# A new hand order for batch 0 of a fused attention and MLP kernel, with small jobs on other engines

## The chip, the cores and the metric

The kernel runs on one core of a Trainium2 chip. The metric is the device time of one execution in microseconds. A core has five instruction streams: TensorE (PE in the profile, its weight loads PEld), VectorE (DVE), ScalarE (ACT), GpSimd (POOL) and SyncE (SP, which here only issues DMAs). Each works through its own queue in order and waits on semaphores for the others. ACT and POOL issue DMAs as well.

## The reference

Eight batches of attention (8 heads, 576 positions, head size 64) with a band of 32 positions to each side and 8 global positions, followed by a residual MLP over the 512 features:

```python
def _attn_ref(q, k, v, global_idx):
    ...
    scores = scale * np.matmul(q, k.transpose(0, 1, 3, 2))
    mask = np.abs(pos[:, None] - pos[None, :]) <= window
    mask = mask | is_global[:, None] | is_global[None, :]
    scores = np.where(mask, scores, -1000000000.0)
    ...
    return np.matmul(attn, v)

def _moe_ref(x, alpha1, beta1, w_tok, alpha2, beta2, w_ch1, w_ch2, lam):
    a1 = alpha1 * x + beta1
    tok = np.einsum('ts,bsd->btd', w_tok, a1)
    u = x + lam * tok
    a2 = alpha2 * u + beta2
    ch = np.maximum(a2 @ w_ch1, 0.0) @ w_ch2
    return u + lam * ch
```

All inputs and the output are float32; the indices are whole numbers.

## The kernel before

The 8 x 576 rows make nine groups of 512 rows for the channel MLP. The first is batch 0's rows 0 to 511. While TensorE runs the MLP of group g, the attention and the token mixing of the next batch are woven between its matmuls at fixed places (`weave`). Batch 0 has no MLP to hide in. Its attention and token mixing come first, as a list of some 190 named steps in the string `FIRST` (line 45), written in the order in which they are issued. A step may carry the number of its PSUM bank, as in `tk0:1`. The order of the string is the order of each engine's queue: a step waits for everything before it on the same engine. The order and the engines were found by a solver outside the kernel; nothing in the kernel decides them at run time. The table `ops` (line 916) says what a step does, and the strings `CK, QV, KC, QC, NY, PZ` (line 915) give the engine of a family of steps for each pair of heads (A is ACT, D is DVE, P is POOL).

The steps that matter here, h being a pair of heads:

- `ck`, `cq`: cast k and q of batch 0 from float32 to bfloat16 (lines 618, 621); `tk`, `tq`: transpose them on TensorE; `kt`, `qv`: copy them from PSUM. `tt`, `ktt`, `qtt`: the same for the last 64 positions.
- `V0` to `V4` (POOL, line 220): loads of the five overlapping chunks of V of batch 0 into `Ve[0]`; `va1`, `vb1`, `va2`, `vb2`: copies shifted by 64 partitions into `Vo[0]`. `u0` to `u4`: the loads of V for batch 1.
- `vez`: three small fills of `Ve[0]`; `v1f`: fills of `Ve[1]` and `KT[1]` for batch 1; `pz`: zero fills of the probability tiles; `qz0`, `qz1`: zero fills of the padded query tile `QP` of batch 1, 64 partitions by 1296 float32 each; `fz`, `ktz`, `pgz`, `kgz`: other fills.
- `s`, `e`: scores and their exponentials (line 361); `pg`, `pt`: masked probabilities (lines 323, 330); `q`, `ra`, `rd`: the rows of the global positions, on TensorE, ACT (line 383) and DVE (line 387); `pvx`, `pvy`: probabilities by V on TensorE, which need `rd`; `nx`, `nr`, `ny`: division by the row sums; `xl`, `xm`: multiplication by alpha1, on POOL for pairs 0 to 2 and on DVE for pair 3.
- `la`, `lb`, `lc`: lam times alpha1, spread over the partitions; `beta`: lam times beta1 in one row (line 860).
- `wki`, `wi`: loads of w_tok and w_ch1 (POOL); `wt`, `we`: transposes of w_tok and their copies; `rs`, `re`: its row sums.
- `tm`, `ad`, `tx`, `ut`: token mixing of one pair, its residual sum (DVE), transposes, and the scaled copy (ACT, line 901) that the channel MLP reads.
- `W1s`: the first nine matmuls of the first MLP group.
- `kc`, `qc`: casts of k and q of batch 1 (lines 618, 621); `gc1`: the global columns of batch 1 in `KGP` and `QP` (lines 242, 248).
- `gat1` (`ld_const`, line 731): SP copies two numbers out of `Ve[0]` into `A2`. The copy has no use as data, but SP waits in it until that chunk of V has landed. Then SP issues four loads of batch 1, k heads 0 to 3, q heads 0 to 3, k heads 4 to 7, q heads 4 to 7 (line 613), into the place where batch 0's k and q stood.
- `sp:n`: n matmuls without use.

After the string, `first_attention(1)` is woven into the first group: transposes of pair 0 of batch 1 (line 632), copies into `QP` by DVE (line 642) and into `KT` by ACT (line 636), the tail, pair 1, then score units, with MLP matmuls between. The PSUM banks 5, 6 and 7 are used in turn, so the pair 1 transposes of q wait for pair 0's copies, and so on.

Of the kernel before, what the change touches and what calls it, by code (L numbers as in the profile page):

```python
# [9 lines left out]
FP32 = mybir.dt.float32  # L10
# [6 lines left out]
P = 128  # L17
S = 576
D = 64
H = 8  # L20
HP = 4
# [3 lines left out]
NW = 9  # L25
# [18 lines left out]
]  # L44
FIRST = """
kgz vez io ktz pgz gb1 gbm:0 W0 gbc ar0 pz1 ar1 gath ck0 ar2 pgc tk0:1 sp:3 cq0 mask idn tq0:2 sp:16 V0 pz3 GM
qv0 V1 pz2 cq1 V2 tq1:3 kt0 cq2 V3 tq2:4 sp:1 ck2 qv1 qv2 ck1 tk2:5 V4 kt2 ck3 tk1:6 wki cq3 gat1 kt1 tk3:0 wi
kt3 gx tq3:2 ct qv3 gt:1 tt:3 sp:3 ge0 gte fz ktt ge1 qtt z20:4 s20:5 gk1:6 e201 la e200 z21:0 z11:2 s11:1
gk0:3 b1t eg1 va1 s21:5 e111 z00:4 s00:6 eg0 z10:1 sp:2 va2 e210 s10:3 vb1 G e211 z01:0 sp:2 e001 s01:5 e100
lb:6 e011 pz0 e010 pg2 z31:1 s31:5 lc v1f pt2 ab:0 sp:2 e310 q2:6 e000 u0 wt1:1 ra2 wt3:4 sp:2 we1 pg0 u1 rd2  # L50
pvx2:6 e101 vb2 pt0 e311 u2 pvy2:1 e110 q0:3 nx2 we3 wt0:5 u3 pg1 ra0 wt2:2 nr2 ny2 we0 wt4:6 xl2 rd0 we2 q1:4
pt1 z30:1 s30:5 pvx0:3 we4 xm2 pvy0:2 nx0 ra1 rs:6 e300 beta rd1 e301 nr0 pg3 pvy1:1 re pvx1:3 ny0 pt3 xl0
q3:4 tm2:5 ra3 nr1 ny1 rd3 xm0 nx1 pvy3:6 pvx3:2 ad2 xl1 tm0:4 nx3 xm1 nr3 ad0 ny3 tx2:3 u4 tm1:5 xl3 b1i xm3
tx0:4 ad1 tm3:6 abe ut0 qz0 ut2 tx1:5 ad3 qz1 ut1 tx3:4 gc1 ut3 W1s qc1 kc1 qc0 kc0 qc3 kc2 kc3 qc2
"""
PLACE = {t: (g, j) for g, ts in enumerate(GROUPS) for j, t in enumerate(ts)}

# [41 lines left out]
def kernel(ctx, tc, q, k, v, global_idx, alpha1, beta1, w_tok, alpha2, beta2, w_ch1, w_ch2, lam, out):  # L99
    nc = tc.nc  # L100
# [8 lines left out]
    def T(name, shape, dt):  # L109
        return cp.tile(list(shape), dt, name=name)  # L110
# [14 lines left out]
    def mm(o, l, r, st, sp):  # L125
        nc.tensor.matmul(out=o, lhsT=l, rhs=r, start=st, stop=sp, skip_group_check=True)  # L126
# [14 lines left out]
    QP = T("QP", [P, HP, 2, NW, 72], BF16)  # L141
    Vef = [T(f"Ve{i}", [P, 5 * H * 65], FP16) for i in range(2)]
    Ve = [t.rearrange("p (c h e) -> p c h e", c=5, h=H) for t in Vef]
    Vo = [T(f"Vo{i}", [P, 4, H, 65], FP16) for i in range(2)]
# [5 lines left out]
    G = T("G", [P, 2, 704], FP16)  # L150
    GM = T("GM", [P, 2, S], FP16)
# [14 lines left out]
    mask = T("mask", [P, NW, 64], FP16)  # L166
    gqm = T("gqm", [P, 5, 8], FP16)
    LA1 = T("LA1", [P, DM], FP32)
    LAM = T("LAM", [P, DM], FP32)
    A2 = T("A2", [P, DM], FP32)  # L170
# [12 lines left out]
    gbc = T("gbc", [P, 8], FP32)  # L183
# [113 lines left out]
    def gk0_mm(ps, t0, nt):  # L297
        for hp in range(HP):
            o = ps[:, 0 : 64 * nt].rearrange("p (t j) -> p t j", j=64)
            mm(o, KGP[:, hp, :], Q0[:, hp, t0 : t0 + nt, 0:64], hp == 0, hp == HP - 1)  # L300
# [305 lines left out]
    def fill(ap, val=0.0, eng=None):  # L606
        (eng or nc.vector).memset(ap, val)
# [4 lines left out]
    def ld_kq(src, st_, eng, b, h0, h1):  # L612
        eng.dma_start(
            out=st_[:, h0:h1, :, :].rearrange("p h j d -> p h (j d)"), in_=src[b, h0:h1, 0:512, :].rearrange("h (p j) d -> p h (j d)", j=4)
        )
# [53 lines left out]
    def tail_k(ps, b):  # L669
        tv = ps.bitcast(BF16)[:, 0:512].rearrange("p (i t) -> p i t", i=4)  # L670
        nc.scalar.copy(out=KT[b % 2][:, :, 544:608], in_=tv[:, :, 0:64])
# [7 lines left out]
    def tail_q0(ps, copy):  # L679
        tv = ps.bitcast(BF16)[:, 0:512].rearrange("p (i t) -> p i t", i=4)  # L680
        copy(out=Q0[:, :, 8, 0:64], in_=tv[:, :, 64:128])
# [31 lines left out]
    zero = nc.const_aps.tensor(0.0, (P, 1), FP32)  # L713

    g_ = nc.gpsimd
# [13 lines left out]
    nc.sync.dma_start(out=abr[4:8, :], in_=alpha2.rearrange("(c p) -> c p", p=P))  # L729

    def ld_const():
        nc.sync.dma_start(out=A2[0:1, 0:1], in_=Ve[0][0:1, 3, 0, 0:2].bitcast(FP32))
        for h0 in (0, 4):
            ld_kq(k, KST, nc.sync, 1, h0, h0 + 4)
            ld_kq(q, QST, nc.sync, 1, h0, h0 + 4)
        for t_, src in ((A2, alpha2), (LAM, lam)):
            nc.sync.dma_start(out=t_, in_=src.unsqueeze(0).to_broadcast([P, DM]))
# [2 lines left out]

    def qzero(a, eng):
        r = slice(64 - 64 * a, 128 - 64 * a)
        fill(QP.rearrange("p h a t j -> p h a (t j)").bitcast(FP32)[r, :, a, :], 0.0, eng)

    def ld_w2(blk):
        g_.dma_start(out=W2[:, 8 * blk : 8 * blk + 8, :], in_=w_ch2[1024 * blk : 1024 * blk + 1024, :].rearrange("(c p) e -> p c e", p=P))
# [14 lines left out]
    def ve_fill(i, eng=g_):  # L761
        fill(VF[i][0:32, 0:260], 0.0, eng)
        fill(VF[i][96:128, 1040:1300], 0.0, eng)
        fill(Ve[i][:, :, :, 64:65], 1.0, eng)

    def kt_fill(i, eng):
        fill(KT[i][:, :, 0:32], 0.0, eng)
        fill(KT[i][:, :, 608:672], 0.0, eng)
# [89 lines left out]
    def b0_beta(par, eng):  # L858
        r = 64 if par == 0 else 0
        eng.tensor_tensor(out=XL4[par][r : r + 1, :], in0=LB[r : r + 1, :], in1=LR[r : r + 1, :], op=ALU.mult)  # L860
# [45 lines left out]
    def ab_ev(ps):  # L906
# [4 lines left out]
    V_ = nc.vector  # L911
    mlp0 = mlp(0)
    hb = {}
    CPY = {"A": nc.scalar.copy, "D": nc.vector.tensor_copy, "P": nc.gpsimd.tensor_copy}
    CK, QV, KC, QC, NY, PZ = "AAAD", "ADDD", "AAAA", "AAAA", "AADA", "PAAA"
    ops = {
        "idn": lambda: nc.scalar.copy(out=ident, in_=identb),
        "kgz": kz_fill,
        "qz1": lambda: qzero(1, g_),
        "W0": warm,  # L920
        "ct": lambda: nc.scalar.copy(out=TSB, in_=TST),
        "gc1": lambda: gcols(1),
        "ktz": lambda: kt_fill(0, V_),
        "qz0": lambda: qzero(0, g_),
        "pgz": pg_zero,
        "vez": lambda: ve_fill(0, V_),
        "io": lambda: g_.iota(out=C16, pattern=[[1, S]], base=0, channel_multiplier=0, allow_small_or_imprecise_dtypes=True),
        "va1": lambda: CPY["D"](out=Vo[0][0:64, 0:3], in_=Ve[0][64:128, 0:3]),
        "vb1": lambda: CPY["P"](out=Vo[0][64:128, 0:3], in_=Ve[0][0:64, 1:4]),
        "va2": lambda: CPY["D"](out=Vo[0][0:64, 3], in_=Ve[0][64:128, 3]),  # L930
        "vb2": lambda: V_.tensor_copy(out=Vo[0][64:128, 3], in_=Ve[0][0:64, 4]),
        "gat1": ld_const,
        "wki": ld_wt,
        "wi": ld_w,
# [18 lines left out]
        "GM": gm,  # L953
        "la": lambda: V_.tensor_tensor(out=LA1[0:1, :], in0=LA1[0:1, :], in1=LR[0:1, :], op=ALU.mult),
        "lb": lambda ps: mm(ps, one_f, LA1[0:1, :], True, True),
        "lc": lambda: nc.scalar.copy(out=LA1, in_=hb["lb"]),
        "beta": lambda: b0_beta(0, g_),
        "tt": tail_tr,
        "ktt": lambda: tail_k(hb["tt"], 0),
        "qtt": lambda: tail_q0(hb["tt"], nc.vector.tensor_copy),  # L960
        "gk0": lambda ps: gk0_mm(ps, 0, 4),
        "gk1": lambda ps: gk0_mm(ps, 4, 5),
        "eg0": lambda: gk_ev(hb["gk0"], 0, 256),
# [182 lines left out]
```

## Time and profile before

| | us |
|---|---|
| median of 5 runs | 389.6 |
| lowest, highest | 389.27, 391.23 |
| profiled execution, its own time | 389.77 |
| its span, first to last instruction | 388.0 |

Mean granted TensorE clock 0.994. Busy time in the span: PE 372.5 us (96%), DVE 227.1 (59%), ACT 175.2 (45%), POOL 209.6 (54%). A few stretches of the start, by engine (busy us of 5):

| stretch | PE | DVE | ACT | POOL |
|---|---|---|---|---|
| 20 to 25 | 4.46 | 4.27 | 5.00 | 4.81 |
| 25 to 30 | 4.03 | 4.81 | 2.58 | 3.87 |
| 30 to 35 | 5.00 | 4.69 | 1.66 | 3.96 |
| 35 to 40 | 3.92 | 2.57 | 5.00 | 4.43 |
| 40 to 45 | 3.45 | 3.28 | 4.59 | 4.37 |
| 45 to 50 | 4.95 | 3.80 | 4.78 | 0.15 |

A matmul's end is modelled, so busy times of PE are upper bounds. Times inside a timeline count from the first instruction. A group's line such as `L618 ACT CAST UT<-XR` gives the source line, the engine, the operation, and the tile written and read; several tiles share memory, so batch 1's cast k appears under `UT` and its cast q under `OT`. "Idle before" names what ended the idle time in front of a group.

### The profile page before, as it was taken

Reading aid. Unit: us, or ns where it says so; the run is one execution under the profiler, and the core shown is the slowest. Engines: PE = TensorE matmul, PEld = TensorE weight load, DVE = VectorE, ACT = ScalarE, POOL = GpSimd, SP = SyncE. Lnnn points to the kernel's source line nnn. Section 1 sums busy time; section 2 is a strip of 40 time slices with the busy share of each in tenths; the row PEclk is TensorE's granted clock in tenths of the full one; section 3 lists DMA queues with packets and bytes.
Section 4 is the critical chain, followed back from the end, with each engine's and each line's share of the span. In section 5 each row is a group of like instructions: output and inputs, shape, how many; then the busy total and the mean of one; then the engine's idle time right before and its main releaser. Section 6 shows DMA issues by size and latency. Waiting matters only on the chain.

```text
span 388.0 us, 8144 instructions
## 1 busy us (share of the span) xinstructions
PE 372.5 (96%) x3067; PEld 209.3 (54%) x3120; DVE 227.1 (59%) x584; ACT 175.2 (45%) x351; POOL 209.6 (54%) x272
## 2 busy tenths in 40 slices
PE   6889799999999999999999999999999999999996
PEld 3468566646654565456545664466446654444443
DVE  7888657785477456945495559545865554014023
ACT  6776975008810782057404840286028700730820
POOL 7997549378649943894378737963241335000000
PEclk9999899999999999999999999999999999999999
DMA  8999999959989995999697999798140013101002
GB/s 254 178 226 268 207 182 133 155 133 169 145 141 134 150 148 101 135 144 138 128 122 127 150 149 95 129 171 159 41 96 28 3 56 81 42 15 67 29 27 81
DMA packets 160836, 47.87 MB, mean 123 GB/s; under 512 B 147537, under 2 KB 154521, under 8 KB 160798
## 3 DMA queue, kind: packets, MB, share of 16 engines
q0 software_dynamic: 98288, 17.05, 61.2%
q1 hardware_dynamic: 61678, 29.71, 37.9%
q10 hardware_dynamic: 832, 0.60, 0.5%
q8 instruction: 24, 0.39, 0.5%
q14 instruction: 14, 0.11, 0.1%
HBM read 38.90 MB, written 9.44 MB: 125 GB/s over the span
## 4 chain that ended last, share of the span: by engine, by line
PE 89%; DVE 5%; ACT 2%; issue 1%; DMA 1%; ACTq 0%; DVEq 0%
PE bank L126 88%; DMA XR<-in_q_dram 1%; PE bank L632 1%; ACT OT L621 1%; DVE PT L330 1%; ACT UT L901 1%; ACT UT L618 1%; DVE XR L426 1%; DVE PGQ L323 0%; DVE W L648 0%; DVE XR L580 0%; DVE OT L579 0%; DVE GM L854 0%; DVE Kb L621 0%; ACT KT L636 0%
## 5 line engine op out<-in xcount | busy, mean ns | idle before, releaser
L126 PE MATMUL bank<-UT,W 128*128 128x512 bf16 x546 | 153.5, 381 | 1.1
L126 PE MATMUL bank<-W,HT 128*128 128x512 bf16 (+2 forms) x573 | 137.3, 373 | 0.9 <-issue 0.2
L564 ACT ACTIVATE HT<-bank,bias 128x512 bf16<-128x512 f32 x128 | 87.9, 687 | 52.4 <-PE bank L126 51.6
L365 ACT ACTIVATE E<-bank 128x416 f16<-128x416 f32 (+1 forms) x84 | 41.7, 514 | 116.4 <-PE bank L126 114.9
L126 PEld LDWEIGHTS <-HT 128*128 128x128 bf16 (+1 forms) x610 | 54.4, 98 | 54.1 <-issue 1.9
L444 POOL TENSOR_TENSOR XL<-XR,LA 128x384 bf16<-128x384 f32 x31 | 31.1, 1004 | 72.8 <-DVE XR L426 52.7
L126 PEld LDWEIGHTS <-W 128*128 128x128 bf16 (+1 forms) x658 | 51.6, 98 | 25.4 <-issue 0.2
L579 DVE TENSOR_TENSOR OT<-bank,LAM 128x512 f32<-128x512 f32 (+2 forms) x37 | 24.9, 674 | 55.3 <-PE bank L126 55.1
L505 POOL TENSOR_TENSOR UB<-XR,A 128x512 bf16<-128x512 f32 x28 | 35.8, 1286 | 22.6 <-DVE XR L500 19.3
L126 PE MATMUL bank<-RG,G 128*128 128x65 f16 x320 | 43.1, 193 | 0.7 <-DVE RG L387 0.4
L126 PE MATMUL bank<-XL,wtT 128*128 128x512 bf16 (+2 forms) x237 | 41.3, 326 | 0.1
L126 PE MATMUL bank<-Ve,PT 128*128 128x65 f16 x300 | 41.2, 194 | 0.0
L126 PEld LDWEIGHTS <-PT 128*128 128x128 f16 x540 | 30.9, 98 | 16.5
L126 PEld LDWEIGHTS <-G 128*128 128x128 f16 x320 | 30.7, 97 | 15.8 <-DVE RG L387 0.9
L220 POOL DMA_DIRECT2D Ve<-in_v_dram x40 | 34.2, 872 | 0.2
L126 PEld LDWEIGHTS <-KT 128*128 128x128 bf16 (+1 forms) x324 | 23.3, 98 | 19.4 <-issue 3.1
L126 PE MATMUL bank<-Vo,PT 128*128 128x65 f16 x240 | 33.4, 192 | 0.0
L213 POOL DMA_DIRECT2D Kb<-in_k_dram x30 | 26.9, 896 | 6.4 <-DMA W<-in_moe_w_ch_dram 5.3
L126 PE MATMUL bank<-QP,KT 128*128 128x144 bf16 (+1 forms) x252 | 28.9, 224 | 0.2
L213 POOL DMA_DIRECT2D Qb<-in_q_dram x30 | 26.8, 892 | 4.2 <-DMA W<-in_moe_w_ch_dram 3.6
L126 PEld LDWEIGHTS <-wtT 128*128 128x128 bf16 (+1 forms) x240 | 18.8, 99 | 17.4 <-issue 1.7
L580 DVE TENSOR_TENSOR XR<-OT,XR 128x512 f32<-128x512 f32 (+2 forms) x33 | 27.0, 817 | 1.6
(160 smaller groups left out, 412.5 us busy)
## 6 DMA issues: line engine op xcount, KB each, us to landing
out_dram<-XR SPq DMA_DIRECT2D x31, 256.0 KB
W<-in_moe_w_ch_dram POOLq DMA_DIRECT2D x4, 1024.0 KB, 17.1
Vo<-Ve SPq DMA_DIRECT2D x14, 260.0 KB
Ve<-in_v_dram POOLq DMA_DIRECT2D x24, 128.0 KB, 5.5
Kb<-in_k_dram POOLq DMA_DIRECT2D x24, 128.0 KB, 6.3
Qb<-in_q_dram POOLq DMA_DIRECT2D x24, 128.0 KB, 6.8
Ve<-in_v_dram POOLq DMA_DIRECT2D x16, 96.0 KB, 5.1
XR<-in_k_dram SPq DMA_DIRECT2D x2, 512.0 KB
```

The costliest lines, as they stand in the source:

```text
L126: nc.tensor.matmul(out=o, lhsT=l, rhs=r, start=st, stop=sp, skip_group_check=True)
L213: nc.gpsimd.dma_start(out=dst[0:n, c, :].rearrange("p (h d) -> p h d", d=D), in_=src[b, :, c * P : c * P + n, :].rearrange("h p d -> p h d"))
L220: nc.gpsimd.dma_start(out=Ve[b % 2][r0 : r0 + hi - lo, c, :, 0:D], in_=v[b, :, lo:hi, :].rearrange("h p d -> p h d"))
L330: nc.vector.tensor_tensor(out=bass.AP(pt.tensor, pt.offset + 64 + 128 * par, [p0, [256, n], [1216, 2], [1, 64]]), in0=bass.AP(e.tensor, e. ...
L365: nc.scalar.activation(out=eb(b, hp)[:, UOFF[u] : UOFF[u + 1]], in_=ps[:, 0:n], func=AF.Exp, bias=0.0, scale=0.125)
L426: nc.vector.tensor_tensor(out=xo, in0=pv[:, :, :, 0:64], in1=rb, op=ALU.mult)
L444: xl_eng(b, hp).tensor_tensor(out=XL[b % 2][:, 0:3, cs], in0=XR[:, base : base + 3, cs], in1=lb, op=ALU.mult)
L505: nc.gpsimd.tensor_tensor(out=ub, in0=x, in1=A2, op=ALU.mult)
L564: nc.scalar.activation(out=HT[:, ec, :], in_=st[ec], func=AF.Relu, bias=b_, scale=1.0)
L579: nc.vector.tensor_tensor(out=ot, in0=ps, in1=LAM[:, lo:hi], op=ALU.mult)
L580: nc.vector.tensor_tensor(out=x, in0=ot, in1=x, op=ALU.add)
L618: copy(out=KB0[:, :, 128 * hp : 128 * hp + 128].rearrange("p j (a d) -> p a j d", a=2), in_=KST[:, 2 * hp : 2 * hp + 2, :, :])
```

## The change

The string `FIRST` is replaced by another order. Some steps go to another engine: `pz0` and `vb1` from POOL to DVE, `pz3` from ACT to DVE, `vez` from DVE to POOL, `qz1` from POOL to ACT, `qz0` from POOL to DVE, `lc` from ACT to DVE, `beta` from POOL to DVE, `qtt` and `qv1` from DVE to ACT, `ny1`, `qc2` and `qc3` from ACT to DVE. `qzero` learns to use ACT, by copying a zero. The gate of `gat1` reads chunk 4 of V instead of chunk 3.

In the new order the pairs of heads run 2, 1, 0, 3 instead of 2, 0, 1, 3. The casts `kc` and `qc` of batch 1, which stood behind `W1s`, are spread among the last steps of batch 0. `v1f` stands ahead of `V4`, and `W1s` ahead of `ad3`, `gc1`, `tx3` and `ut3`.

```diff
-kgz vez io ktz pgz gb1 gbm:0 W0 gbc ar0 pz1 ar1 gath ck0 ar2 pgc tk0:1 sp:3 cq0 mask idn tq0:2 sp:16 V0 pz3 GM
...
-q3:4 tm2:5 ra3 nr1 ny1 rd3 xm0 nx1 pvy3:6 pvx3:2 ad2 xl1 tm0:4 nx3 xm1 nr3 ad0 ny3 tx2:3 u4 tm1:5 xl3 b1i xm3
-tx0:4 ad1 tm3:6 abe ut0 qz0 ut2 tx1:5 ad3 qz1 ut1 tx3:4 gc1 ut3 W1s qc1 kc1 qc0 kc0 qc3 kc2 kc3 qc2
+kgz pgz pz0 gb1 ktz gbm:0 io W0 gbc ar0 pz2 vez ar1 idn gath ck0 GM pgc tk0:1 sp:9 ck1 ar2 V0 kt0 tk1:2 sp:2
+cq1 pz1 V1 mask tq1:3 sp:5 ck2 cq2 V2 kt1 tk2:4 pz3 qv1 tq2:5 sp:3 V3 ck3 kt2 qv2 tk3:6 sp:8 v1f qz1 cq3 V4
+cq0 gat1 tq3:0 kt3 gx tq0:1 wki ct qv3 gt:2 qv0 wi tt:3 sp:1 ge0 gte ge1 ab:4 ktt la z10:5 z20:6 s20:0 s10:1
...
+we4 xl2 pvx1:1 nr2 ny2 we1 q0:0 nx1 xm2 z30:5 s30:3 ra0 rs:2 e301 rd0 e300 xl1 nr1 ny1 pvy0:1 e310 beta re xm1
+pvx0:0 nr0 kc1 pg3 tm2:3 ny0 pt3 q3:5 qc1 xm0 nx0 tm1:4 ra3 kc2 rd3 xl0 kc0 ad2 pvx3:6 ad1 qc0 pvy3:2 tm0:5
+kc3 b1i nr3 nx3 ny3 xl3 tx1:3 ad0 tx2:4 ut1 xm3 tx0:6 ut2 qc3 tm3:5 qc2 ut0 qz0 W1s ad3 gc1 tx3:3 ut3

-        nc.sync.dma_start(out=A2[0:1, 0:1], in_=Ve[0][0:1, 3, 0, 0:2].bitcast(FP32))
+        nc.sync.dma_start(out=A2[0:1, 0:1], in_=Ve[0][0:1, 4, 0, 0:2].bitcast(FP32))

     def qzero(a, eng):
...
+        if eng is nc.scalar:
+            eng.copy(out=z, in_=bass.AP(zero.tensor, zero[r].offset, [zero[r].ap[0], [0, HP], [0, NW * 36]]))
+        else:
+            fill(z, 0.0, eng)

-    CK, QV, KC, QC, NY, PZ = "AAAD", "ADDD", "AAAA", "AAAA", "AADA", "PAAA"
+    CK, QV, KC, QC, NY, PZ = "AAAD", "AADD", "AAAA", "AADD", "ADDA", "DAAD"
...
-        "qz1": lambda: qzero(1, g_),
+        "qz1": lambda: qzero(1, nc.scalar),
-        "qz0": lambda: qzero(0, g_),
+        "qz0": lambda: qzero(0, V_),
-        "vez": lambda: ve_fill(0, V_),
+        "vez": lambda: ve_fill(0, g_),
-        "vb1": lambda: CPY["P"](out=Vo[0][64:128, 0:3], in_=Ve[0][0:64, 1:4]),
+        "vb1": lambda: CPY["D"](out=Vo[0][64:128, 0:3], in_=Ve[0][0:64, 1:4]),
-        "lc": lambda: nc.scalar.copy(out=LA1, in_=hb["lb"]),
-        "beta": lambda: b0_beta(0, g_),
+        "lc": lambda: V_.tensor_copy(out=LA1, in_=hb["lb"]),
+        "beta": lambda: b0_beta(0, V_),
-        "qtt": lambda: tail_q0(hb["tt"], nc.vector.tensor_copy),
+        "qtt": lambda: tail_q0(hb["tt"], nc.scalar.copy),
```

More of the change, by code (lines that the diff above doesn't have):

```diff
@@ L45 @@
 FIRST = """
-kgz vez io ktz pgz gb1 gbm:0 W0 gbc ar0 pz1 ar1 gath ck0 ar2 pgc tk0:1 sp:3 cq0 mask idn tq0:2 sp:16 V0 pz3 GM
[L47 to L52, printed above, removed]
-q3:4 tm2:5 ra3 nr1 ny1 rd3 xm0 nx1 pvy3:6 pvx3:2 ad2 xl1 tm0:4 nx3 xm1 nr3 ad0 ny3 tx2:3 u4 tm1:5 xl3 b1i xm3
-tx0:4 ad1 tm3:6 abe ut0 qz0 ut2 tx1:5 ad3 qz1 ut1 tx3:4 gc1 ut3 W1s qc1 kc1 qc0 kc0 qc3 kc2 kc3 qc2
+kgz pgz pz0 gb1 ktz gbm:0 io W0 gbc ar0 pz2 vez ar1 idn gath ck0 GM pgc tk0:1 sp:9 ck1 ar2 V0 kt0 tk1:2 sp:2
+cq1 pz1 V1 mask tq1:3 sp:5 ck2 cq2 V2 kt1 tk2:4 pz3 qv1 tq2:5 sp:3 V3 ck3 kt2 qv2 tk3:6 sp:8 v1f qz1 cq3 V4
+cq0 gat1 tq3:0 kt3 gx tq0:1 wki ct qv3 gt:2 qv0 wi tt:3 sp:1 ge0 gte ge1 ab:4 ktt la z10:5 z20:6 s20:0 s10:1
+qtt va1 z00:2 e200 lb:3 b1t e201 abe e100 vb1 z11:6 s11:4 fz lc e101 z01:0 z21:5 sp:2 e110 gk0:1 vb2 e111
+s21:3 eg0 z31:6 pg1 s31:4 e211 gk1:1 e210 u0 pt1 e311 s00:3 s01:5 eg1 pg2 u1 q1:4 e011 va2 q2:1 G e010 wt0:5
+u2 ra2 wt3:0 pt2 e000 u3 e001 wt1:2 rd2 ra1 wt2:3 pt0 u4 we0 pvx2:1 we2 rd1 wt4:5 nx2 pvy1:4 we3 pg0 pvy2:3
+we4 xl2 pvx1:1 nr2 ny2 we1 q0:0 nx1 xm2 z30:5 s30:3 ra0 rs:2 e301 rd0 e300 xl1 nr1 ny1 pvy0:1 e310 beta re xm1
+pvx0:0 nr0 kc1 pg3 tm2:3 ny0 pt3 q3:5 qc1 xm0 nx0 tm1:4 ra3 kc2 rd3 xl0 kc0 ad2 pvx3:6 ad1 qc0 pvy3:2 tm0:5
+kc3 b1i nr3 nx3 ny3 xl3 tx1:3 ad0 tx2:4 ut1 xm3 tx0:6 ut2 qc3 tm3:5 qc2 ut0 qz0 W1s ad3 gc1 tx3:3 ut3
 """
@@ L742, in qzero @@
         r = slice(64 - 64 * a, 128 - 64 * a)
-        fill(QP.rearrange("p h a t j -> p h a (t j)").bitcast(FP32)[r, :, a, :], 0.0, eng)
+        z = QP.rearrange("p h a t j -> p h a (t j)").bitcast(FP32)[r, :, a, :]
+        if eng is nc.scalar:
+            eng.copy(out=z, in_=bass.AP(zero.tensor, zero[r].offset, [zero[r].ap[0], [0, HP], [0, NW * 36]]))
+        else:
+            fill(z, 0.0, eng)
     def ld_w2(blk):
```

## The prediction

> **What bounds the kernel now.** I read the page's slices, then the chain of waits, then the timelines of the first 50 us by engine, then the DMA view cut into short stretches. In the slices TensorE is near full from the sixth on; in the chain of waits everything after 47.6 us is TensorE on line 126, one piece after another with 0.05 us between. What the change can win or lose lies before that: the time at which TensorE becomes full. The chain of waits there:
>
> ```profile
> 35.00 2.09 ACT UT L901 x3
> ...
> 37.74 0.61 ACT OT L621
> 38.35 0.52 ACT UT L618
> 38.87 0.52 ACT OT L621
> ...
> 42.52 0.59 PE bank L632 x4
> ...
> 47.60 5.59 PE bank L126 x43
> ```
>
> Columns: start, length, engine, tile, line. The reader is to see ScalarE (ACT) casting batch 1's q and k one after the other (`qc`, `kc`, lines 618 and 621, eight times 0.52 us) between the end of batch 0 and the first transposes of batch 1. By stretches, with TensorE's busy time first and its granted clock after the five engines:
>
> ```profile
> 37.10:42.30 5.20, 3.29 (x24) 1.67 (x24) 2.36 (x4) 5.20 (x11) 4.69 (x7) 1.00 2.19 177
> 42.30:45.70 3.40, 3.18 (x19) 2.17 (x19) 2.46 (x5) 2.99 (x8) 2.27 (x3) 0.50 1.25 208
> 45.70:47.40 1.70, 1.65 (x18) 1.16 (x18) 0.97 (x3) 1.55 (x4) 0.00 (x0) 0.99 1.19 270
> ```
>
> ACT is full for 5.2 us while TensorE runs few matmuls, then TensorE has 3.4 us at half clock. Between 39.05 (end of `W1s`) and 49.48 the timeline has 8 pair transposes (0.22 each), a tail (0.22), 6 score units (0.19) and 14 MLP matmuls (0.216): 6.1 us of work in 10.4. So 4.3 us is the most that this stretch can give.
>
> **Why the casts stood there.** Their data come late. The four batch 1 loads (512 KB, 512 packets each, line 613) are behind a gate: SP's tiny copy on line 732 waits for a V chunk of batch 0.
>
> ```profile
> 15.39 0.72 SPq L732 DMA_DIRECT2D A<-Ve  x1
> ...
> 17.86 9.48 SPq L613 DMA_DIRECT2D XR<-in_q_dram  x1
> ```
>
> POOL's timeline has the V loads of batch 0 and the fills that will matter below:
>
> ```profile
> 6.63 4.56 POOL L220 DMA_DIRECT2D Ve<-in_v_dram  x5
> ...
> 18.71 1.01 POOL L607 MEMSET Ve<- 32x260 f32 x3
> 19.51 0.57 POOL L607 MEMSET KT<- 128x128 bf16 x2
> ```
>
> The DMA view of 20 to 28 us, then of 30 to 32 (queue, packets, MB, share of an engine's time):
>
> ```profile
> q0 software_dynamic: 365, 1.43, 88.1%
> q1 hardware_dynamic: 359, 0.37, 16.5%
> ```
> ```profile
> q1 hardware_dynamic: 490, 0.49, 87.9%
> q0 software_dynamic: 486, 0.06, 46.0%
> ```
>
> The two queues get the same number of packets. While the 4 KB packets of W1 (POOL's queue, q0) run, the 1 KB packets of q and k (q1) move 45 packets a us; once W1 is through, 245. Adding q1's packets over the stretches (359 to 28, 662 to 30, 1152 to 32, 1644 to 34, 2096 to 36) the loads pass 512, 1024, 1536 and 2048 at about 29.0, 31.5, 33.5 and 35.8; the last landing marks in the trace, which are the slowest DMA engine's, are 30.3 (k, heads 0-3), 32.5 (q, heads 0-3), 34.65 (k, heads 4-7), 37.0 (q, heads 4-7). Before, nothing waits for these: the first cast is at 37.74.
>
> **The change, part by part.**
>
> *Engines.* Durations of one, old engine to new: `pz0` POOL 0.63 to DVE, `pz3` ACT 0.72 to DVE (not shown; by the DVE memset of 256 f32 in 0.27, 1.05 ns a column, 640 columns give 0.67); `vez` DVE 0.73 to POOL 1.01; `vb1` POOL 1.48 to DVE 0.56 (row of line 928, same shape); `beta` POOL 1.34 to DVE 0.88 (line 860's own DVE row at 72.79); `lc` ACT 0.58 to DVE 0.69 (line 894); `qv1` DVE 0.65 to ACT 0.58; `qtt` DVE 0.29 to ACT 0.39; `ny1` ACT 1.02 to DVE 0.56; `qc2`, `qc3` ACT 0.61 to DVE 0.43 each; `qz0` POOL 1.17 to DVE 1.36 (1296 columns at 1.05); `qz1` POOL 1.17 to ACT 1.27 (640 columns in 0.71, 320 in 0.44, so 0.84 ns a column more). Sums: DVE +0.67+0.67-0.73+0.56+0.88+0.69-0.65-0.29+0.56+0.86+1.36 = +4.6 us; ACT -0.72-0.58+0.58+0.39-1.02-1.22+1.27 = -1.3; POOL -0.63+1.01-1.48-1.34-2.34 = -4.8. Part of DVE's comes back, since POOL work beside it had stretched it (line 323 at 27.40: 1.28 for two against 0.30; line 275: 1.72 against 0.83 at 52.11): some 2 us. None of this sets the end by itself: DVE gets to head pair 3's `pg3` at 27.5 to 28.5 by my sum, against 27.4 before. If the relief did not come it would be 2 us, hidden behind the wait below up to about 30.
>
> *POOL's queue.* `v1f` (1.01 + 0.57 = 1.58 us) now stands ahead of the last V chunk, `vez` ahead of the gathers (they go from 4.07 to 4.33). So `V4` is issued at 6.9 + 3.85 + 1.58 = 12.3 instead of 10.4, and w_tok and W1, behind it, 1.9 us later. V chunks landed 5.5 us after issue, one by one in step with their issues, so nothing is queued in front that would hide this.
>
> *SP's queue.* The gate now waits for chunk 4: 12.3 + 5.5 = 17.8 instead of 15.4 (chunk 3). The four loads are issued 2.4 us later, but were slowed by W1 anyway, which moves by up to 1.9. Bounds for the shift of the landings: 0 (W1 still ends when it did and the loads catch up at 245 packets a us) and 2.4; between them nearer W1's move, I take 1.6. Landings then: 31.9, 34.1, 36.2, 38.6.
>
> *ACT's queue, the term that decides.* `kc1` now stands before `ny0`, `qc1` before `ra3`, `kc2 kc0 qc0 kc3` before `ny3` and the four `ut`. ACT's work ahead of `kc1` is no longer than before, where the last of it (`re`) ended at 27.5. It reaches `kc1` at 27 to 28 and must wait. Step by step: `kc1` 31.9 to 32.4, `ny0` (0.82) to 33.3, `qc1` 34.1 to 34.6, `ra3` 34.9. Behind `ra3` wait `rd3` on DVE, and behind that in DVE's queue `ad2` and `ad1`, and on TensorE `pvx3 pvy3 tm0`. Then `kc2` 36.2 to 36.75, three casts to 38.3, `ny3` 39.1. Behind it DVE's `xm3` 39.7; `tm3` 41.0 on TensorE; `W1s` 41.0 to 42.9 (before 37.16 to 39.05). On DVE behind `xm3`: `qc3 qc2` 40.4, `qz0` 41.8, `ad3` (0.69) 42.5, `gc1` (1.9 as at 36.17) 44.4, pair copies of line 642 for head pair 0 (1.39) 45.8, tail (0.59) 46.4, pair 1 47.8. The pair 2 k transposes wait for the bank that this copy frees: 47.8 against 44.95 before. From there TensorE's own order (items 12 to 16, two score units: 1.5 us) takes it to the pair 3 k transposes at 49.4 against 47.21.
>
> *Sum.* 49.4 - 47.2 = +2.2 us. With the landing shift at 0 the same walk ends +0.7, with 2.4 at +2.9.
>
> *The clock.* One stretch of 3.41 us at 0.50 stands in the trace; a score unit of three took 0.55 us in it against 0.34 after. The new wait leaves TensorE from about 30.5 to 35 with next to nothing, and another from 43.8 to 45.8. A second such stretch costs between 0 (over a wait) and 1.7 us (full of work); I take 0.4, since most of the work behind waits for other engines.
>
> The Trainium skill (TensorE: Matmul & The Clock Gate, "What's actually happening") says that the clock falls to half after an idle window of about 3.4 us and comes back after as long a busy one. The trace agrees in the length, 3.41 us. By that rule a new half-clock stretch behind the wait is certain rather than possible, and it would fall on `tm0` (1.28 us to 2.56), so the sum would be +3.5 instead of +2.6.
>
> Total: +2.6 us. The profiled execution took 389.77 (span 388.0 and 1.8 around it), the median of five is 389.6 (389.27 to 391.23); on the median, **392.2**. Own range of this case, 0.7 to 2.9 plus 0 to 1.7: 390.3 to 394.2. What a measurement of this kernel can tell from no change is about 0.5%, 1.95 us.
>
> **Rivals.**
>
> *The casts find their data (faster).* Place: `kc1` on ACT. If k had landed by 28, none of the waits above exist: `rd3` at 29.8, `xm3` 33.8, `tm3` 35.1, `W1s` to 37.1, `qc3 qc2 qz0 ad3 gc1` to 38.5, pair copies 39.9, 40.5, 41.9, and the pair 3 transposes at 43.6 instead of 47.4: -3.8, 385.8. For it: ACT is busy only 2.58 of 5 us from 25 to 30 and 1.66 from 30 to 35, so the casts have room there, and the stretch behind is worth 4.3. It decides below landings some 3 us earlier than before. Against: they land at 30.3 to 37.0 and the gate moves later.
>
> *The waits are there but cost little (within 0.5%).* W1 doesn't move, because the DMA engines had a backlog: +0.7 to +1.9, 390.3 to 391.5. For: the DMA share from 10 to 15 us is 3.31, so packets did stand in line. Against: V landed in step with issue.
>
> *DVE becomes the bound.* Its 4.6 us more with no relief put `pg3` at 30 and everything behind it later by up to 2, so that the waits only partly hide it: 393.5 and above. For: DVE was busy 4.8 of 5 from 25 to 30. Against: POOL's contention falls.
>
> **How the numbers follow.** Forecast 0.52, DVE bound 0.08: slower 0.60. Waits that cost little 0.27: same. Casts find their data, or another gain that I don't see, 0.13: faster. The range leaves out most of the faster case and the top of the DVE case, some 0.18 in all: 388.4 to 394.6.
>
> **What would show it.** Right: ACT idle before a line 618 cast around 28 to 32, put down to the XR loads; line 387's last one at about 35; first MLP matmuls near 41; line 732's copy at 17 to 18. Wrong: casts of line 618 running back to back with no DMA before them, or `W1s` before 37, or V chunk 4 landing by 16.

## The result, and the profile after

| | before | after |
|---|---|---|
| median, us | 389.81 (79 runs) | 393.03 (42 runs) |
| lowest, highest | 388.42, 393.93 | 391.59, 394.69 |
| span of the profiled execution | 388.0 | 391.7 |
| mean granted TensorE clock | 0.994 | 0.991 |

The ratio is 1.0077 (95% interval 1.0066 to 1.0088): the changed kernel is slower by 3.2 us. Lines from 745 on stand 4 higher than before (901 is now 905, 860 is 864, 894 is 898).

ScalarE's timeline of the changed kernel (start, length, engine, line, operation, out<-in; in brackets the idle time ahead of it and what ended it):

```profile
27.74 0.58 ACT L885 CAST wtT<-bank 1x512 bf16<-1x512 f32 x1
33.18 0.62 ACT L618 CAST UT<-XR 128x512 bf16<-128x512 f32 x1 [4.87 <-DMA XR<-in_k_dram]
...
35.31 0.62 ACT L621 CAST OT<-XR 128x512 bf16<-128x512 f32 x1 [0.59 <-DMA XR<-in_q_dram]
35.83 0.36 ACT L383 ACTIVATE RG<-bank,C 128x130 f16<-128x130 f32 x1
37.49 1.14 ACT L618 CAST UT<-XR 128x512 bf16<-128x512 f32 x2 [1.29 <-DMA XR<-in_k_dram]
...
40.37 2.10 ACT L905 ACTIVATE UT<-bank,b2f,a2c 128x512 bf16<-128x512 f32 x3
```

ACT is through with the row sums of w_tok (`re`) at 28.3 and then stands 4.87 us before `kc1`. A load leaves sixteen landing marks in the trace, one for each DMA engine. The first casts start within 0.03 us of the last mark of their loads, 33.16, 35.28, 37.47 (before: 30.95, 33.07, 35.25). Line 383 at 35.83 is `ra3`, work of batch 0: its input was ready at 33.2 (line 126 on `PGQ` at 32.46, in TensorE's timeline below), but it is queued behind two casts.

VectorE's timeline shows who waits for it:

```profile
27.84 3.20 DVE L864 TENSOR_TENSOR XL<-UB 1x512 bf16<-1x512 f32 x1
...
36.23 0.30 DVE L387 SCALAR_TENSOR_TENSOR RG<-bank,RG 32x130 f16<-32x130 f32 x1 [3.20 <-ACT RG L383]
...
41.77 1.14 DVE L607 MEMSET QP<- 64x1296 f32 x1 [0.31 <-issue]
42.94 0.69 DVE L898 TENSOR_TENSOR XR<-bank,XR 128x512 f32<-128x512 f32 x1
...
45.32 1.39 DVE L642 COPY QP<-bank 64x512 bf16<-64x512 bf16 x2 [1.14 <-PE bank L632]
```

`rd3` (line 387) waits 3.20 us for `ra3`. Then TensorE's timeline:

```profile
31.18 1.49 PE L126 MATMUL bank<-XL,wtT 128*128 128x128 bf16 x16 [2.19 <-DVE XL L864]
32.46 0.75 PE L126 MATMUL bank<-Ve,PGQ 128*128 128x130 f16 x5
...
40.35 1.55 PE L126 MATMUL bank<-XL,wtT 128*128 128x128 bf16 x20
42.52 2.10 PE L126 MATMUL bank<-UT,W 128*128 128x512 bf16 x8 [0.62 <-DMA Ve<-in_v_dram]
...
46.77 0.38 PE L632 MATMUL bank<-C,OT 128*128 128x128 bf16 x4 [1.03 <-DVE QP L642]
...
53.23 2.12 PE L126 MATMUL bank<-QP,KGP 128*128 128x256 bf16 x16
55.19 1.24 PE L126 MATMUL bank<-UT,W 128*128 128x512 bf16 x5
56.49 0.45 PE L126 MATMUL bank<-Ve,PGQ 128*128 128x130 f16 x5
```

`W1s` starts at 42.52 (37.16 before). The idle time ahead of it is put down to a V load, but ACT's `ut` on line 905 ends at 40.37 + 2.10 = 42.47: that is what it waited for. The products with `KGP` start at 53.23 against 49.48, those with `PGQ` at 56.49 against 52.74: 3.75 us later both, and the spans differ by 3.7 (the profiled execution of after took 393.65, 0.6 above the median). So the whole loss has arisen by here and nothing of it is given back. The chain of waits names other work:

```profile
18.56 22.48 DMA Ve<-in_v_dram
...
41.30 15.15 DMA KQG<-in_q_dram,hidx
...
56.49 3.73 PE bank L126 x40
```

That is not the cause: TensorE's timeline just above shows MLP matmuls up to 56.43 without a gap. The chain followed the last semaphore back through loads that cost nothing. Its shares are no guide here; the engines' timelines are.

The same stretches of 3.40 us (busy time of the five engines, then the granted clock):

```profile
18.00:21.40 3.40, 3.40 (x46) 1.92 (x44) 3.26 (x11) 2.28 (x8) 3.40 (x6) 0.50 1.12 214
28.20:31.60 3.40, 1.13 (x22) 0.83 (x19) 3.34 (x5) 0.11 (x1) 3.15 (x6) 1.00 1.11 234
31.60:35.00 3.40, 3.40 (x36) 3.40 (x34) 1.40 (x4) 1.52 (x5) 0.59 (x2) 0.50 1.33 272
35.00:38.40 3.40, 2.08 (x50) 1.96 (x48) 2.11 (x6) 1.80 (x4) 2.60 (x4) 0.99 1.34 290
```

There are two half-clock stretches, at 18.0 to 21.4 and at 31.6 to 35.0. The second lies over the casts' wait. But the idle time of TensorE ahead of it, 2.19 us in the window of 28.2 to 31.6, was ended by `beta` on DVE (the row at 31.18 above), not by a load.

Why the loads come later is seen in the timelines of SP's queue and of POOL:

```profile
15.58 0.72 SPq L732 DMA_DIRECT2D A<-Ve  x1
```
```profile
10.20 1.09 POOL L607 MEMSET Ve<- 32x260 f32 x3
11.08 0.57 POOL L607 MEMSET KT<- 128x128 bf16 x2
11.59 0.78 POOL L220 DMA_DIRECT2D Ve<-in_v_dram  x1
12.36 0.87 POOL L779 DMA_DIRECT2D HT<-in_moe_w_tok_dram  x1
13.22 1.42 POOL L783 DMA_DIRECT2D W<-in_moe_w_ch_dram  x2
...
26.51 0.78 POOL L220 DMA_DIRECT2D Ve<-in_v_dram  x1 [4.53 <-DMA W<-in_moe_w_ch_dram]
```

The gate (line 732) opens only 0.2 us later than before: V chunk 4 landed 4.0 us after its issue. But the fills of `v1f` hold back w_tok and W1 by 1.2 us. Queue q0 in the DMA view of 14 to 18 us, first before, then after (packets, MB, share):

```profile
q0 software_dynamic: 787, 0.79, 143.7%
```
```profile
q0 software_dynamic: 613, 0.50, 112.6%
```

The DMA engines moved 0.29 MB less in these 4 us. W1 landed at 26.2 and 33.0 (before 24.4 and 30.5), and the batch 1 loads, which get packet for packet what W1's queue gets, moved with it. The DMA view of 20 to 28 us after:

```profile
q0 software_dynamic: 371, 1.43, 88.5%
q1 hardware_dynamic: 348, 0.36, 16.1%
```

Mark for mark, the last landings of the four loads moved by 2.2 to 2.3 us.

### The profile page after: what moved, and what is told of

It reads as the page before. It is cut to its first block, busy times and chain, and to the rows that moved or that the text cites. A ratio compares the mean times of both kernels' runs of the same rounds, so it can differ in the third digit from the quotient of the medians.

```text
span 391.7 us, 8135 instructions
## 1 busy us (share of the span) xinstructions
PE 374.5 (96%) x3066; PEld 212.0 (54%) x3119; DVE 229.7 (59%) x589; ACT 174.1 (44%) x346; POOL 205.6 (52%) x270
## 4 chain that ended last, share of the span: by engine, by line
PE 85%; DMA 10%; POOL 1%; issue 1%; ACT 1%; DVE 1%; ACTq 0%
PE bank L126 84%; DMA Ve<-in_v_dram 6%; DMA KQG<-in_q_dram,hidx 4%; PE bank L632 0%; DVE XR L580 0%; DVE OT L579 0%; POOL W L783 0%; POOL TSB L624 0%; ACT L739 0%; ACT KT L636 0%; ACTq L613 0%; POOL XL L607 0%; PE bank L267 0%; POOL wtT L607 0%; DVE XR L426 0%
## 5 line engine op out<-in xcount | busy, mean ns | idle before, releaser
L444 POOL TENSOR_TENSOR XL<-XR,LA 128x384 bf16<-128x384 f32 x31 | 31.4, 1014 | 71.6 <-DVE XR L426 47.4
L126 PE MATMUL bank<-XL,wtT 128*128 128x512 bf16 (+2 forms) x237 | 43.1, 337 | 2.5 <-DVE XL L864 2.2
L126 PEld LDWEIGHTS <-PT 128*128 128x128 f16 x540 | 30.9, 98 | 16.7
L126 PEld LDWEIGHTS <-wtT 128*128 128x128 bf16 (+1 forms) x240 | 20.1, 105 | 20.2 <-issue 4.5
```

Source lines behind the costliest of these rows:

```text
L444: xl_eng(b, hp).tensor_tensor(out=XL[b % 2][:, 0:3, cs], in0=XR[:, base : base + 3, cs], in1=lb, op=ALU.mult)
```

## The experiments

Theories: **W** (ACT's casts wait for late loads, with batch 0's work queued behind them), **D** (DVE's longer queue sets the end), **C** (half clock), **A** (the small transpose `ab`, moved ahead of the first scores, waits on TensorE for two small loads). The kernel before was measured again with each group of runs: its median was 390.70 us beside the first four runs below, 389.86 beside the next four and 389.63 beside the last four. So the ratios are to be compared, not the times.

**Without the four loads.**

```diff
-        for h0 in (0, 4):
-            ld_kq(k, KST, nc.sync, 1, h0, h0 + 4)
-            ld_kq(q, QST, nc.sync, 1, h0, h0 + 4)
```

> The changed kernel without the four loads of batch 1's q and k; its casts then read what batch 0 left in the same place, and batch 1's result is not the reference's. Theory W (the casts on ACT wait for these loads and hold the rest of batch 0 behind them): no cast waits, the idle time before lines 618 and 621 goes from 6.8 us to under 0.5, and the time falls by 3 to 5 us, to 388 to 390. Theory D (VectorE's added work sets the end, above all beta, 3.20 us): within 1 us of the changed kernel, 392 to 394. Theory C (the two half-clock stretches of TensorE cost the time): the stretch at 18 to 21 us stays, 391 to 392.

> The kernel before, with the same four loads left out, as a control; batch 1's result is not the reference's. W: nothing waits for these loads before the change, so 389.8 within 1 us. If the loads cost time by loading the DMA engines alone, whatever the order, it falls by 2 us or more, to below 388.

Measured: after without loads 0.9986 (0.9952 to 1.0020) of before, before without loads 0.9986 (0.9959 to 1.0014). The loads cost before nothing that can be told, and after everything it lost. ACT's timeline of after without loads has no wait on a DMA ahead of the casts:

```profile
28.29 0.62 ACT L618 CAST UT<-XR 128x512 bf16<-128x512 f32 x1
...
31.55 0.62 ACT L621 CAST OT<-XR 128x512 bf16<-128x512 f32 x1
```

W predicts this. D falls as the main cause: DVE's queue was as long here (`beta` 2.71 us). C falls with it: both half-clock stretches are still there, the second at the same time as in after, and the loss is gone. TensorE's timeline and a stretch of the same run:

```profile
30.65 1.06 PE L126 MATMUL bank<-XL,wtT 128*128 128x128 bf16 x16 [1.98 <-DVE XL L861]
```
```profile
31.60:35.00 3.40, 3.40 (x42) 3.40 (x40) 2.36 (x6) 3.00 (x7) 2.65 (x4) 0.50 2.23 155
```

The faster rival of the prediction falls in part too: with the data there at 28 the time is that of before, not 385.8. What batch 0 waits for then is `beta`: TensorE stands 1.98 us for it, the half clock follows, and `W1s` starts at 39.32 (before 37.16).

**`v1f` behind POOL's early loads** (also with `u0` to `u4` late).

```diff
-tk3:6 sp:8 v1f qz1 cq3 V4
+tk3:6 sp:8 qz1 cq3 V4
...
-lb:3 b1t e201 abe
+lb:3 b1t v1f e201 abe
```

> The changed kernel with the fills v1f moved behind b1t in POOL's queue, so that V4, w_tok and W1 are issued 1.5 us earlier. W: the four landings (33.2, 35.3, 37.5, 39.7) come 1.5 to 2.8 us earlier, the first waiting cast ends as much earlier, and the time falls by 1.5 to 2.5 us, to 390.5 to 391.5. D: unchanged, 393. C: unchanged, 393.

> As the run before it, and the loads u0 to u4 of batch 1's V moved behind xl0 in POOL's queue, so that their 128-byte packets don't share the DMA engines with the q and k loads. From 30 us on the q and k loads then move at 300 or more packets a us instead of 245. W: the last landing at 34 to 36 us, the time falls another 1 to 3 us, to 388 to 390. D: at most the part of beta that POOL stretched, 391.5 to 393. C: 393.

Measured, `v1f` late: 1.0026 (1.0002 to 1.0051); the landings came at 31.77, 33.72, 35.90 and 38.05 (of this last load one mark isn't in the trace), 1.4 to 1.6 us earlier than in after, and ACT waited 3.5 us for them instead of 6.8. So a part of the loss goes when 1.58 us of fills leave POOL's early queue: two thirds by this ratio, less by a later run with `v1f` late (below, 1.0063); the profiled span of both is 1.5 to 1.6 us shorter than after's, of 3.7 lost. With the V loads late as well: 1.0048 (1.0016 to 1.0079), a miss. The first cast started no earlier (34.29): fifteen of the load's sixteen marks were there at 31.38, the last at 34.27. In that profile TensorE also stood 3.9 us at `ab`, whose input came late, and had half clock from 16.9 to 27.2. What the V loads alone do stays open.

**Same loads, same engines, other order.** ACT's work of batch 0 goes ahead of the casts:

```diff
-kc1 pg3 tm2:3 ny0 pt3 q3:5 qc1 xm0 nx0 tm1:4 ra3 kc2 rd3 xl0 kc0 ad2 pvx3:6 ad1 qc0 pvy3:2 tm0:5
-kc3 b1i nr3 nx3 ny3 xl3 tx1:3 ad0 tx2:4 ut1 xm3 tx0:6 ut2 qc3 tm3:5 qc2 ut0 qz0 W1s ad3 gc1 tx3:3 ut3
+pg3 tm2:3 ny0 pt3 q3:5 xm0 nx0 tm1:4 ra3 kc1 rd3 xl0 ad2 pvx3:6 ad1 qc1 pvy3:2 tm0:5 b1i nr3 nx3 ny3 kc0
+xl3 tx1:3 ad0 tx2:4 qc0 ut1 xm3 tx0:6 ut2 tm3:5 ut0 kc2 qz0 W1s ad3 gc1 kc3 tx3:3 qc2 ut3 qc3
```

> The changed kernel with the same loads and the same engines; only the last stretch of the order is laid out anew, so that ny0 and ra3 stand ahead of the first cast, ny3 ahead of kc0 and qc0, the three ut ahead of kc2, and kc3, qc2, qc3 behind gc1. The data land as late as before (33 to 40 us). Theory W: batch 0's steps no longer stand behind casts that wait, the first MLP matmuls start 2 to 3 us earlier, and the time falls by 2.5 to 4 us against the changed kernel, to 389 to 390.5 in the terms of the first measurement (ratio to before 0.998 to 1.002). Theory D: VectorE has the same work, no change, ratio 1.007. Theory C: the half-clock stretch at 18 to 21 us stays, the one at 31.6 to 35 goes, ratio 1.004 to 1.006.

Measured: 1.0014 (0.9999 to 1.0028). The landings are as late as in after (33.21, 35.40, 37.52, 39.74). ACT's timeline:

```profile
33.23 0.62 ACT L618 CAST UT<-XR 128x512 bf16<-128x512 f32 x1 [0.51 <-DMA XR<-in_k_dram]
35.42 0.62 ACT L621 CAST OT<-XR 128x512 bf16<-128x512 f32 x1 [1.57 <-DMA XR<-in_q_dram]
...
37.77 2.12 ACT L905 ACTIVATE UT<-bank,b2f,a2c 128x512 bf16<-128x512 f32 x3
```

The first cast starts at the same time as in after, but `ut` ends 2.6 us earlier and the `KGP` products start at 50.65 instead of 53.23. So it isn't the late data by itself that costs, but what stands behind the casts on ACT. This shows W with both of its conditions: the same lateness is nearly free in this order, and in after's order the time follows the landings.

**`ab` behind the global rows.**

```diff
-ge0 gte ge1 ab:4 ktt
+ge0 gte ge1 ktt
...
-e201 abe e100
+e201 e100
...
-q2:1 G e010
+q2:1 ab:7 G abe e010
```

> The changed kernel with the transpose ab, which waits for two small loads (abr, 4 rows of 512 bytes each), moved from before batch 0's first scores to behind q2, into bank 7, and abe behind G. TensorE waited 0.5 us for abr in the changed kernel's profile, 2.1 to 3.9 us in three runs of variants. W: the stretch behind is held by the landings anyway, so at most 0.5 us, ratio 1.006 to 1.008. A theory that this wait is the cost of the change (theory A): 2 us or more, ratio below 1.002.

> v1f moved behind b1t as in the earlier run, and ab moved as in the run before. W: like the earlier run with v1f alone (ratio 1.0026), at most 0.5 us below it, since the casts still wait: 1.001 to 1.003. Theory A: 2 us below, 0.998.

Measured: 1.0094 (1.0070 to 1.0117) and 1.0063 (1.0035 to 1.0090). No gain from moving `ab`, so A falls: what `ab` holds up on TensorE early on is still done before the casts' data land. Mark for mark, the loads land 0.7 us earlier in the second run than in the first.

**All together, and beyond.** `best1` puts `v1f` and `ab` late, `u4` behind the token mixing and the casts in the new order. `best1_sp` adds spare matmuls, `best2` moves `beta` and `qz0` back to POOL (and to behind `u3` in the string), `best3` puts pair 0's transposes of batch 1 ahead of `W1s`, `best3_sp` has both.

```diff
 best1_sp, on best1:
-tt:3 sp:1 ge0
+tt:3 sp:3 ge0
...
-s20:0 s10:1
+s20:0 sp:4 s10:1
...
-e200 lb:3
+e200 sp:3 lb:3
 best2, on best1:
-    "beta": lambda: b0_beta(0, V_),
-    "qz0": lambda: qzero(0, V_),
+    "beta": lambda: b0_beta(0, g_),
+    "qz0": lambda: qzero(0, g_),
 best3, on best2 (t0 before W1s, tm3 in bank 7):
+    "t0": lambda: tr_pair(1, 0)[1](),
-        a = [t_[0], tr_tail(b), gap(0.5),
+        a = [tr_tail(b), gap(0.5),
```

> All of it: v1f and ab late, u4 back in front of b1i (it held POOL's queue for 3 to 4.5 us while W1 landed), and the casts laid out anew. W: batch 0 runs without a wait for q and k, landings at 31.3 to 37.6, first MLP matmuls near 36.5, attention of batch 1 right behind: ratio 0.990 to 0.995, 386 to 388. D: VectorE's extra 4.6 us set the end, ratio 1.000 or above.

> The re-laid kernel with nine more spare matmuls (256 columns, results unused) at 12.8 to 16.2 us, where TensorE waited in pieces of 0.3 to 0.7 us and after which it had half clock for two stretches of 3.4 us (16.2 to 23.0). Theory that the half clock there delays batch 0: no half clock at 16 to 23, the first PGQ products and pg3 0.5 to 1 us earlier, ratio 0.995 to 0.997. Rival, that other engines' work hides it: the clock changes, the time doesn't, 0.997 to 1.000. If the stretch comes all the same, the spares are too few and the run says nothing.

> The re-laid kernel with beta and qz0 back on POOL, in its idle stretch at 22.5 to 26 us, as DVE was nearly full from 22.8 to 38.9. Theory that DVE sets the end there (beta 1.15 and qz0 1.14 on its queue): pair copies of line 642 start 1 us earlier than at 40.34, ratio 0.994 to 0.996. Rival, that TensorE's order (pair 0 behind W1s and tx3) and ACT's casts set it: DVE gets idle time instead, 0.997 to 0.999.

> The same as best2, and the pair 0 transposes of batch 1 stand before W1s instead of behind W1s and tx3. If these copies behind W1s were the last wait: the first line 642 copy before 38.5 instead of 40.3, gk_all about 1 us earlier than in best2, ratio 0.991 to 0.995. Rival, that the later pairs wait for ACT's or DVE's copies anyway: no more than 0.3 us against best2.

> best3 with the nine spares of best1_sp: the sum of both if they are independent, 0.989 to 0.994; no better than best3 if the clock's stretch is hidden behind other engines.

| | ratio to before | median, us | `KGP` products start |
|---|---|---|---|
| best1 | 0.9982 (0.9966 to 0.9998) | 389.07 | 48.25 |
| best1_sp | 1.0002 (0.9978 to 1.0025) | 389.54 | 48.87 |
| best2 | 0.9979 (0.9960 to 0.9998) | 389.24 | 48.66 |
| best3 | 1.0022 (1.0000 to 1.0043) | 390.76 | 51.78 |
| best3_sp | 1.0004 (0.9981 to 1.0028) | 390.26 | 49.81 |

`best1` and `best2` are faster than both kernels, but by only 0.2% against before, and I had expected 0.5 to 1%. None of the four steps beyond `best1` brought what was expected of it. The spares did remove the half clock, as stretches of `best1` and then `best1_sp` show:

```profile
18.00:21.40 3.40, 3.40 (x46) 1.99 (x45) 2.50 (x9) 2.06 (x7) 3.34 (x7) 0.50 1.06 216
```
```profile
18.00:21.40 3.40, 3.25 (x67) 2.48 (x66) 3.29 (x16) 3.30 (x11) 3.34 (x7) 1.00 1.10 220
```

Batch 0 came through up to 1.8 us earlier (`beta` at 26.81 instead of 28.62), and the gain was lost at once, in ACT's timeline of `best1_sp`:

```profile
31.47 0.62 ACT L618 CAST UT<-XR 128x512 bf16<-128x512 f32 x1 [1.61 <-DMA XR<-in_k_dram]
33.65 0.62 ACT L621 CAST OT<-XR 128x512 bf16<-128x512 f32 x1 [1.56 <-DMA XR<-in_q_dram]
```

The loads had become the floor: a faster batch 0 waits for them again. So half clock is real in these kernels, but its removal didn't shorten the time. In `best2`, DVE was relieved of 2.3 us and idle instead. In `best3_sp` the first pair copies come at 37.61 (40.34 in `best1`), but the next ones at 43.51 (42.39), as `W1s` and DVE's casts now stand between. `best3` by itself ran at half clock for four stretches, from about 16.7 to 30.3, in its profile, so only `best3_sp` can be read for its step.

## Why the prediction was right

The prediction was 392.2 with a range of 388.4 to 394.6 and 0.60 on slower; 393.03 was measured. The mechanism was the one forecast, and the runs show it: the casts wait for loads, and `ra3`, `rd3`, `ny3`, `ut` and `W1s` stand behind them. By its steps:

| step | before | forecast | after |
|---|---|---|---|
| last landing marks of k 0-3, q 0-3, k 4-7, q 4-7 | 30.95, 33.07, 35.25, 37.39 | 31.9, 34.1, 36.2, 38.6 | 33.16, 35.28, 37.47, 39.66 |
| `rd3` starts | 29.84 | 35 | 36.23 |
| `W1s` starts | 37.16 | 41.0 | 42.52 |
| first pair copies | 39.95 | 44.4 | 45.32 |
| pair 3 k transposes | 47.21 | 49.4 | 50.69 |

- **The landings were the mis-sized term**: they came 1.1 to 1.3 us later than forecast. Half of that is a misreading: 30.3, 32.5, 34.65 and 37.0 are the fourteenth of each load's sixteen marks, and the last ones stand 0.4 to 0.6 later. The other half is the shift, 2.2 to 2.3 us where I took 1.6, inside the bounds of 0 to 2.4. Its working failed at the gate: I had V land 5.5 us after issue and so the gate 2.4 us later; it moved 0.2. V chunk 4 had landed at 15.6, and "landing by 16" was one of the signs that I had named for being wrong. The delay came by another way, through w_tok and W1, which were held back 1.2 us and landed 1.8 to 2.5 us later, with less moved at 14 to 18 us. I had named W1's move as the nearer bound, but sized it by the issue times. The walk of the prediction rises by 0.9 us for each us of landing; 1.3 us on top of its 2.2 makes 3.3, and the pair 3 transposes came 3.5 later, the medians 3.2.
- **`gc1` was too dear**: 1.9 us taken from rows that POOL's fill beside it had stretched; 0.63 after, with `qz0` off POOL. `qz0` took 1.14 instead of 1.36. Only part of these 1.5 us came through, since DVE then waits 1.14 us for the transposes behind `W1s`: `W1s` is 1.5 us later than forecast, the first pair copies 0.9, the pair 3 transposes 1.3. That these errors and the landings' pull against each other is luck, and part of why 392.2 lies so near.
- **`beta` was too cheap**: 3.20 us instead of 0.88. In after it cost nothing that can be seen, as it ended at 31.04, under the wait for the first load. It is what emptied TensorE ahead of the second half-clock stretch.
- **The clock.** The stretch of half clock came, but over the wait (31.6 to 35.0), not on the work behind it; `tm0` ran at full clock (0.99 from 35.0). My 0.4 us for it wasn't spent there, and before's own slow stretch at 42.3 to 45.7 is gone. The Trainium skill (TensorE: Matmul & The Clock Gate, "What's actually happening") puts the fall after an idle window of about 3.4 us; here TensorE was busy for 1.13 us of the 3.40 before. Length and order agree. But I had the wait for the loads empty TensorE from 30.5 on; it was `beta` that emptied it, from 29.0, and without the loads the stretch came all the same (31.6 to 35.0). So the slow stretch lay under the loads' wait and not behind it, and the +3.5 that I drew from the rule didn't follow.
- **DVE as the bound** was rightly given little, though its sign came: `pg3` at 31.28, where the rival named 30, held by `beta` and hidden by the loads. **Casts that find their data** was half right: without the loads after is as fast as before, so the new order by itself gains nothing, where I had worked out -3.8 us (-3.6 from the row at 47.21, which it took as 47.4). It had `rd3` at 29.8; with `beta` at 2.71 us it came at 32.69.
- **Not seen**: `u4`, moved ahead of `xl2` on POOL, held it 4.53 us until W1 had landed; and `ab` waiting on TensorE (0.49 us in after, up to 3.9 in other runs). In after, both end before the casts' wait does.

## What to carry to other kernels

A job that is moved ahead in an in-order queue brings its own wait along: before moving it, compare the landing of its data with the time at which the queue reaches it, and count everything behind it as late. A fill on the engine that issues DMAs is paid in landings, also of loads on another queue: moving 1.58 us of fills behind POOL's early loads brought SP's last loads 0.7 to 1.6 us forward. A landing is the last of sixteen marks, and the last can come up to 2.9 us behind the fifteenth (the run with `v1f` and the V loads late), so it is read mark for mark. When a kernel is balanced among several floors, as here with loads, ACT's order, DVE and TensorE's order, taking one away uncovers the next within a microsecond.

## What the runs showed of the hardware

**One operation, 1.15 or 3.20 us.** `beta` (one row of 512, two operands in SBUF) took 1.15 to 1.17 us on DVE in six profiles, 2.71 without the loads, 2.76 with `ab` late, 3.20 in after, always beside POOL's products of lines 444 to 462. From `after_v1f_late`, DVE and then POOL:

```profile
29.55 1.15 DVE L864 TENSOR_TENSOR XL<-UB 1x512 bf16<-1x512 f32 x1
```
```profile
28.75 1.00 POOL L444 TENSOR_TENSOR XL<-XR,LA 128x384 bf16<-128x384 f32 x1
29.70 0.46 POOL L461 TENSOR_TENSOR XL<-XR,LA 128x128 bf16<-128x128 f32 x1
30.12 0.90 POOL L462 TENSOR_TENSOR XL<-SR,LA 64x128 bf16<-64x128 f32 x1
```

In each of these runs one of POOL's products took 0.9 us instead of 0.45, and `beta` ended 0.58 us after that one's start (here 30.12 + 0.58 = 30.70). It looks as if `beta` runs for 0.58 us and waits before that: here for the rest of one POOL product and the next, in after for the rest of one and four more. The Trainium skill (SBUF — State Buffer, "SBUF: two separate sides") has DVE and GpSimd hold a shared pair of ports one at a time, for DVE operations with two SBUF inputs beside GpSimd operations that read SBUF, as here; the one that comes second is blocked for the whole instruction of the other. The runs agree that they block each other; that the wait can last over several instructions they show as well, and why it is two in some runs and four or five in others stays open.

**Half clock comes from sparse work too.** In `best1` TensorE was busy for 1.83 of the 3.41 us up to 16.16, and then ran at half clock to 22.99, two stretches. Its busy share was full there: matmuls at half speed fill the time, and only the clock column shows the loss. The busy share alone doesn't tell when it comes: in after 2.50 of 3.41 us (14.56 to 17.98) were followed by half clock, in before 2.19 of 3.41 (11.60 to 15.01) were not.

**An issue can wait for an earlier load.** POOL stood 4.53 us at the issue of `u4`, with `xl2`, an input of the token mixing, behind it. In the trace that issue waits for a semaphore that the first half of W1 signals when it lands (26.23) and that `u4`'s own load uses next. So here the reuse of a semaphore made the wait; whether the DMA queue would have held the issue as well is not shown.
